# Scores of the first batch as plain float32 products, and a later place for VectorE's conversion of three weight pieces

## The chip, the core and the metric

One core of a Trainium2 chip runs the whole kernel. The metric is the device time of one execution in microseconds (us). Its engines are TensorE (PE; its weight loads are PEld), VectorE (DVE), ScalarE (ACT), GpSimd (POOL) and SyncE (SP), which here issues every DMA. Each engine takes its instructions in the order in which they stand in its own queue.

## What is computed

Three stages follow each other: attention with a decay, a gated feed-forward layer, and eight expert layers with a balanced gate.

```python
scores = scale * np.matmul(q, k.transpose(0, 1, 3, 2))      # 4 batches, 8 heads, 576 x 576, head size 64
decay  = cum[:, :, :, None] - cum[:, :, None, :]            # cum: running sum of log f
scores = np.where(causal, -1e9, scores + decay)
attn   = softmax(scores)                                    # max, exp, sum, divide
x      = np.matmul(attn, v)                                 # -> (2304, 512)
x      = (silu(x @ w_gate) * (x @ w_val)) @ w_out           # first feed-forward layer, 512 -> 1536 -> 512
out    = sum over 8 experts e of P[:, e] * (relu(x @ w1[e]) @ w2[e])
```

The change is in the scores of batch 0 and in when a part of `w_gate`, `w_val` and `w_out` is prepared.

## The kernel before

**Order.** The program writes lists of steps (`attn_unit`, `moe_unit`) and `merge` (L21) interleaves two lists by their costs. Then a scheduler puts the instructions of each engine into a fixed order. L475 merges the attention of batch 0 with the conversion of the first three weight pieces; L476 merges the attention of batch 1 with the first feed-forward layer of batch 0, which converts 15 more pieces as it needs them; the later stages follow in the same way. A unit of the feed-forward layer needs all four pairs of heads of its batch, since it sums over 512 features, 128 from each pair.

**A head of attention.** `load` (L227) fetches q and k of one head, transposed, as 64 partitions (head size) by 2 x 576 columns. It fetches them twice, into partitions 0 to 63 and 64 to 127 (L230). ScalarE rounds all of it to the reduced float32 format fp32r (L247, tile `qkh`); GpSimd then replaces the lower half of q by the rest that rounding left (L249), and writes the rest of k to `kl` (L250). So one product over 128 partitions gives (q high + q low) times k high, and a second one with `kl` adds the rest of k. `cb` holds the decay sums, repeated over 128 partitions; that of the very first head is made by TensorE and ScalarE (L238, L241), the others are fetched.

`scores` (L256) takes 128 query rows at a time (five tiles; the last in two chunks of 288 columns). For a chunk TensorE makes the product with `kh` (L268, at least 256 columns wide), adds a causal mask by a bfloat16 product with the identity (L271, on the chunk that ends at the diagonal), and makes the product with `kl` (L272). VectorE adds the decay and takes the minimum in one pass to tile `np` (L274), ScalarE takes the exponential (L278). `trans` (L301) transposes the tile by TensorE (L309), and VectorE or ScalarE copies it out (L313). `pv` multiplies it with v (L332): in batch 0 as plain float32, which shows as two matmul records for each product. `fold` (L346) divides by the sums of a pair of heads: a row goes out to DRAM and comes back repeated (L292, L297), and GpSimd multiplies (L350).

**A weight piece.** `convert` (L98) turns one of 18 pieces of 1 MB, stored as 64-bit floats, into a high and a low fp32r part. A DMA fetches it to `st` (L103; two buffers), VectorE, ScalarE and VectorE again compute on the words (L111, L113, L114, L116, L117: four VectorE steps), GpSimd adds (L122), ScalarE and GpSimd write the two parts to `w` (L124, L142), and a DMA stores them for the later batches (L126). Before the change nothing but the scheduler decides where the four VectorE steps stand among the score rows.

Of the kernel before, what the change touches and what calls it, by code (L numbers as in the profile page):

```python
# [8 lines left out]
F32 = mybir.dt.float32  # L9
F32R = mybir.dt.float32r  # L10
# [10 lines left out]
def merge(*streams, lead=1.0):  # L21

    at = [0.0] * len(streams)
    total = [(sum(c for c, _ in s) or 1.0) * (1.0 if n else lead) for n, s in enumerate(streams)]
    left = [list(s) for s in streams]
    while any(left):
        i = min((at[n] / total[n], n) for n in range(len(left)) if left[n])[1]
        cost, step = left[i].pop(0)
        at[i] += cost
        step()  # L30
# [3 lines left out]
def attention_two_ffns(ctx: ExitStack, tc: tile.TileContext, qkT, vt, f, wf, g2, w1, w2, out):  # L34
    nc = tc.nc
    B, H, D, _, S = qkT.shape
# [4 lines left out]
    P = 128  # L41
# [7 lines left out]
    def pool(name, bufs, **kw):  # L49
        return tc.tile_pool(name=name, bufs=bufs, **kw)  # L50
# [14 lines left out]
    identb = const.tile([P, P], BF16, name="identb")  # L65
# [3 lines left out]
    maskb = const.tile([P, P], BF16, name="maskb")  # L69
# [28 lines left out]
    def convert(i):  # L98
        base = bases[:, 1:2] if i % 3 == 2 else bases[:, 0:1]
        W = 2 * HP  # L100
        st = cvp.tile([P, 4 * W + 4], U16, tag="st", name="st", bufs=2)
        with tc.issue_after(last_qk[0].ins) if i < PACE else ExitStack():
            nc.sync.dma_start(out=st[:, 1:1 + 4 * W], in_=wf[i].bitcast(U16))  # L103

        def words(dt):
            return st.bitcast(dt)[:, 0:2 * W].rearrange("p (i t) -> p i t", t=2)[:, :, 1]
        mid, v = words(U32), words(F32)
        top = st[:, 4:4 + 4 * W].rearrange("p (i t) -> p i t", t=4)[:, :, 0]
        y = cvp.tile([P, W], U16, tag="y", name="y")
        g = cvp.tile([P, W], U16, tag="g", name="g")  # L110
        nc.vector.tensor_scalar(out=y, in0=top, scalar1=0x7fff, scalar2=None, op0=ALU.bitwise_and)  # L111

        nc.scalar.activation(out=g, in_=y, func=AF.Relu, scale=8.0, bias=base)  # L113
        nc.vector.scalar_tensor_tensor(  # L114
            out=g, in0=top, scalar=0x8000, in1=g, op0=ALU.bitwise_and, op1=ALU.bitwise_or)
        nc.vector.tensor_scalar(out=y, in0=g, scalar1=0xff80, scalar2=None, op0=ALU.bitwise_and)  # L116
        nc.vector.scalar_tensor_tensor(  # L117
            out=v, in0=mid, scalar=2.0**-36, in1=y.bitcast(BF16), op0=ALU.mult, op1=ALU.mult)
        t = wring.tile([P, 2, 2, HP], F32R, tag="w", name="w")
        halves = [slice(j * HP, (j + 1) * HP) for j in range(2)]  # L120
        for h in halves:
            nc.gpsimd.tensor_tensor(out=v[:, h], in0=v[:, h], in1=g[:, h].bitcast(BF16), op=ALU.add)  # L122
        for j, h in enumerate(halves):
            nc.scalar.copy(out=t[:, j, 0], in_=v[:, h])  # L124
            rest(t[:, j, 1], v[:, h], t[:, j, 0])
        nc.sync.dma_start(out=wsplit[i], in_=t.bitcast(F32))  # L126
        return t

    last_dma = [None]
    last_qk = [None]  # L130
    NPE = 1
    PACE = 2
    ONV = (2, 4)

    def fetch(i):
        t = wring.tile([P, 2, 2, HP], F32R, tag="w", name="w")
        last_dma[0] = nc.sync.dma_start(out=t.bitcast(F32), in_=wsplit[i])
        return t

    def rest(out, src, hi, eng=None):  # L140

        (eng or nc.gpsimd).tensor_tensor(out=out, in0=src, in1=hi.bitcast(F32), op=ALU.subtract)  # L142
# [14 lines left out]
    raw = at_ctx.enter_context(pool("raw", 2, side="right"))  # L157
    spl = at_ctx.enter_context(pool("spl", 2, side="right"))
# [3 lines left out]
    small = at_ctx.enter_context(pool("small", 1, side="right"))  # L162
# [40 lines left out]

    def attn_unit(b):
        first = b == 0
        pairs, heads = {}, {}

        def load_pair(hp):
            if hp == 0:
# [15 lines left out]
            pairs[hp] = vs, btp.tile([P, S], F32, tag="bt", name="bt", bufs=2)  # L225

        def load(h):  # L227
            qk = raw.tile([P, 2, S], F32, tag="qk", name="qk")
            src = qkT[b, h]
            for half in (slice(0, 64), slice(64, P)):  # L230
                last_qk[0] = nc.sync.dma_start(out=qk[half], in_=src)
            cb = raw.tile([P, S], F32, tag="cb", name="cb")
            r = b * H + h
            if r < NPE:

                for c0 in (0, HB):
                    ps = ps_t.tile([P, 512], F32, tag="t", name="ps_c")
                    nc.tensor.matmul(  # L238
                        out=ps[:, 0:HB], lhsT=ident[0:B * H, r:r + 1].to_broadcast([B * H, P]), rhs=ct[:, c0:c0 + HB],
                        start=True, stop=True)  # L240
                    nc.scalar.copy(out=cb[:, c0:c0 + HB], in_=ps[:, 0:HB])  # L241
            else:
                nc.sync.dma_start(out=cb, in_=cumd[r:r + 1, :].to_broadcast([P, S]))
            qkh = spl.tile([P, 2, S], F32R, tag="qkh", name="qkh")
            kl = spl.tile([P, S], F32R, tag="kl", name="kl")
            a, kh = qkh[:, 0], qkh[:, 1]
            nc.scalar.copy(out=qkh, in_=qk)  # L247

            rest(a[64:128], qk[64:128, 0], a[64:128])  # L249
            rest(kl, qk[:, 1], kh)  # L250
            mn = small.tile([P, 6], F32, tag="mn", name="mn", bufs=4)
            heads[h] = a, kh, kl, cb, mn, {}
            if h % 2 == 0:
                load_pair(h // 2)

        def scores(h, qi):  # L256
            a, kh, kl, cb, mn, nps = heads[h]
            sm, col = sms[h // 2 % 2], (h % 2 * 4 + qi if qi < 4 else 8 + h % 2)
            last = qi == 4
            qs, r0 = (448, 64) if last else (qi * P, 0)  # L260
            L = min((qi + 1) * P, S)
            pt = npp.tile([P, L], F32, tag=f"np{qi}", name="np")
            nps[qi] = pt
            chunks = ((0, 288, 288), (288, 288, 288)) if last else ((0, max(L, 256), L),)
            prev = 3.0e38
            for n, (c0, w, use) in enumerate(chunks):
                ps = (ps_m if first else ps_s).tile([P, 512], F32, tag="m" if first else "s", name="ps_s")
                nc.tensor.matmul(out=ps[:, 0:w], lhsT=a[:, qs:qs + P], rhs=kh[:, c0:c0 + w], start=True, stop=False)  # L268
                if c0 + use == L:
                    m0 = qs - c0  # L270
                    nc.tensor.matmul(out=ps[:, m0:m0 + P], lhsT=identb, rhs=maskb, start=False, stop=False)  # L271
                nc.tensor.matmul(out=ps[:, 0:w], lhsT=a[:, qs:qs + P], rhs=kl[:, c0:c0 + w], start=False, stop=True)  # L272
                m = mn[r0:P, qi + n:qi + n + 1]
                nc.vector.tensor_tensor_reduce(  # L274
                    out=pt[r0:P, c0:c0 + use], in0=ps[r0:P, 0:use], in1=cb[r0:P, c0:c0 + use], scale=-SCALE,
                    scalar=prev, op0=ALU.add, op1=ALU.min, accum_out=m)
                prev = m
            nc.scalar.activation(  # L278
                out=pt[r0:P, 0:L], in_=pt[r0:P, 0:L], func=AF.Exp, scale=-1.0, bias=prev,
                accum_out=sm[r0:P, col:col + 1])  # L280
# [20 lines left out]
        def trans(h, qi):  # L301
# [9 lines left out]
            if first:  # L311
                copy = nc.vector.tensor_copy if qi in ONV else nc.scalar.copy
                copy(out=pts[qi // 2 > 0][h % 2][:, 0:n, c:c + w], in_=pv)  # L313
# [40 lines left out]
        def head_a(h):  # L354
            scores(h, 0)
            scores(h, 1)
            trans(h, 0)
            trans(h, 1)
            pv(h, 0)

        def front_b(h):
            for t in (2, 3, 4):
                scores(h, t)
# [7 lines left out]
        for h in range(H):  # L371
            steps += [(c, lambda fn=fn, h=h: fn(h)) for c, fn in
                      ((0.3, load), (1.5, head_a), (2.0, front_b), (2.0, back_b))]
            if h % 2 == 1:
                steps.append((0.3, lambda hp=h // 2: fold(hp)))
# [3 lines left out]
    def group(w):  # L379
        return [w[0][:, 0], w[1][:, 0]], [w[0][:, 1], w[1][:, 1]], [w[2][:, 0], w[2][:, 1]]  # L380
# [91 lines left out]

    LA, LB, LC = 1.0, 1.2, 1.2
    w0 = []
    merge(attn_unit(0), [(1.0, lambda i=i: w0.append(convert(i))) for i in range(3)])  # L475
    merge(attn_unit(1), moe_unit(0, convert, group(w0)), lead=LA)  # L476
    merge(attn_unit(2), moe_unit(1), lead=LB)
    merge(attn_unit(3), moe_unit(2), lead=LC)
    at_ctx.close()
# [275 lines left out]
```

## Time and profile before

| | |
|---|---|
| median of 3 runs | 2271.68 us (2269.86 to 2273.07) |
| span of the profiled execution | 2267.1 us; its own time is not printed apart from the three runs, whose median lies 4.6 us over the span |
| TensorE busy | 2224.7 us, 98% of the span |
| VectorE, ScalarE, GpSimd busy | 1689.3 us (75%), 852.1 us (38%), 887.4 us (39%) |
| moved by DMA | 232.5 MB, 103 GB/s on average |

The span goes from the first to the last instruction. A busy TensorE is an average over stages: in the first stages, in which attention and conversion run, it has its gaps. A matmul's record is longer than the time after which the next one starts, because matmuls are pipelined; what a matmul costs in a stream is read from one start to the next.

### The profile page before, as it was taken

The numbers are of one execution on the slowest core, as the hardware profiler recorded it, in microseconds if no ns is written. First come the engines' busy times: TensorE is split into PE (matmuls) and PEld (weight loads), VectorE is DVE, ScalarE is ACT, GpSimd is POOL, SyncE is SP. The second block draws the span as 40 slices with busy tenths as digits, with TensorE's granted clock in tenths as the row PEclk, the third lists the DMA queues.
The fourth block names the chain that finished last, engine by engine and source line by source line (L and its number), as shares of the span: only waits on it lengthen the run. The fifth ranks groups of instructions, "written<-read, shape, count | busy, mean of one in ns | idle before, by whom it ended". The sixth has DMA issues, their size and how long they took to land.

```text
span 2267.1 us, 36323 instructions
## 1 busy us (share of the span) xinstructions
PE 2224.7 (98%) x13881; PEld 2020.8 (89%) x13881; DVE 1689.3 (75%) x3385; ACT 852.1 (38%) x1952; POOL 887.4 (39%) x684
## 2 busy tenths in 40 slices
PE   7898999999999999999999999999999999999999
PEld 5698899999999888898988989889989899898897
DVE  6778854544535799887888878877788787887876
ACT  7866754454322434332322323223232232322321
POOL 6869863342423444332323323333233232332320
PEclk9999999999999999999999999999999999999999
DMA  9766664454644232111111111161111111111101
GB/s 249 204 204 217 217 228 159 164 170 146 236 161 154 89 119 94 59 56 38 47 47 38 56 38 47 49 224 56 38 47 47 38 56 38 47 47 38 56 29 52
DMA packets 105102, 232.50 MB, mean 103 GB/s; under 512 B 10672, under 2 KB 60128, under 8 KB 92896
## 3 DMA queue, kind: packets, MB, share of 16 engines
q1 hardware_dynamic: 104928, 230.18, 31.5%
q8 instruction: 109, 1.79, 0.3%
q14 instruction: 65, 0.53, 0.1%
HBM read 193.27 MB, written 36.87 MB: 102 GB/s over the span
## 4 chain that ended last, share of the span: by engine, by line
PE 85%; DMA 6%; DVE 5%; POOL 1%; ACT 1%; issue 1%; SPq 1%; POOLq 0%; DVEq 0%; ACTq 0%
PE py L150 39%; PE pa L601 30%; PE pm L150 10%; DMA st<-wf 3%; PE ps_o L340 1%; PE ps_t L309 1%; PE ps_s L272 1%; DMA xst<-xd 1%; PE ps_s L268 1%; DMA rb<-rd 1%; DVE al L616 1%; DVE np L274 0%; DMA rd<-rt 0%; DVE y L111 0%; DMA lgd<-ls 0%
## 5 line engine op out<-in xcount | busy, mean ns | idle before, releaser
L601 PE MATMUL pa<-xf,w1h 128*128 128x288 f32 x3584 | 748.8, 295 | 0.2 <-DVE u L610 0.2
L601 PEld LDWEIGHTS pa<-xf,w1h 128*128 128x128 f32 x3584 | 597.7, 188 | 37.8 <-DVE u L610 0.7
L653 DVE SCALAR_TENSOR_TENSOR acc<-py,lg,acc 128x512 f32<-128x512 f32 x531 | 395.2, 744 | 247.5 <-PE py L150 247.3
L601 PE MATMUL pa<-xf,w1l 128*128 128x288 f32 x1792 | 527.6, 295 | 0.0
L142 POOL TENSOR_TENSOR w2l<-w,w2h 128x1024 fp32r<-128x1024 f32 x64 | 154.6, 2416 | 820.5 <-ACT w2h L577 820.5
L150 PE MATMUL py<-w2h,ah 128*128 128x512 f32 x1152 | 454.2, 394 | 3.3 <-DVE acc L646 2.8
L150 PE MATMUL py<-w2l,ah 128*128 128x512 f32 x1152 | 454.1, 394 | 0.0
L150 PE MATMUL py<-w2h,al 128*128 128x512 f32 x1152 | 453.2, 393 | 0.0
L616 DVE SCALAR_TENSOR_TENSOR al<-c,ah 128x288 fp32r<-128x288 f32 x512 | 431.5, 870 | 5.4 <-ACT ah L615 4.7
L615 ACT ACTIVATE ah<-c 128x288 fp32r<-128x288 f32 x512 | 208.0, 443 | 566.4 <-PE py L150 319.5
L601 PEld LDWEIGHTS pa<-xf,w1l 128*128 128x128 f32 x1792 | 337.0, 188 | 10.6
L150 PE MATMUL pm<-xh,w 128*128 128x288 f32 x1536 | 326.3, 298 | 3.3 <-DVE xa L431 1.6
L150 PEld LDWEIGHTS py<-w2h,al 128*128 128x128 f32 x1152 | 216.3, 188 | 50.0
L150 PEld LDWEIGHTS pm<-xh,w 128*128 128x128 f32 x1536 | 252.0, 188 | 6.2 <-DVE xa L431 2.1
L150 PEld LDWEIGHTS py<-w2h,ah 128*128 128x128 f32 x1152 | 216.3, 188 | 32.6 <-DVE acc L646 3.2
L150 PEld LDWEIGHTS py<-w2l,ah 128*128 128x128 f32 x1152 | 216.3, 188 | 26.1
L150 PE MATMUL pm<-xl,w 128*128 128x288 f32 x768 | 226.2, 295 | 0.5 <-POOL xl L142 0.5
L621 ACT COPY m<-pa 128x288 f32<-128x288 f32 x128 | 50.3, 393 | 437.0 <-PE pa L601 434.8
L142 POOL TENSOR_TENSOR w1l<-w,w1h 128x256 fp32r<-128x256 f32 x192 | 162.3, 873 | 125.1 <-ACT w1h L573 125.1
L150 PE MATMUL py<-ah,w 128*128 128x288 f32 x768 | 174.6, 299 | 4.8 <-DVE th L413 2.5
L142 POOL TENSOR_TENSOR al<-th,ah 128x288 fp32r<-128x288 f32 x96 | 83.6, 871 | 203.0 <-ACT ah L415 200.7
L142 POOL TENSOR_TENSOR w1l<-sm,w1h 128x1024 fp32r<-128x1024 f32 x64 | 153.7, 2401 | 2.5 <-ACT w1h L573 2.5
(145 smaller groups left out, 3109.4 us busy)
## 6 DMA issues: line engine op xcount, KB each, us to landing
w<-w SPq DMA_DIRECT2D x128, 512.0 KB, 3.5
w<-wsplit SPq DMA_DIRECT2D x54, 1024.0 KB, 5.5
qk<-qkT SPq DMA_DIRECT2D x64, 288.0 KB, 6.2
st<-wf SPq DMA_DIRECT2D x18, 1024.0 KB, 8.7
wsplit<-w SPq DMA_DIRECT2D x18, 1024.0 KB, 4.7
cb<-cumd SPq DMA_DIRECT2D x31, 288.0 KB, 4.0
xo<-h SPq DMA_DIRECT2D x28, 288.0 KB, 2.2
xf<-xo SPq DMA_DIRECT2D x14, 576.0 KB, 10.1
```

The lines of the kernel that those rows point to most:

```text
L142: (eng or nc.gpsimd).tensor_tensor(out=out, in0=src, in1=hi.bitcast(F32), op=ALU.subtract)
L150: nc.tensor.matmul(out=ps, lhsT=a, rhs=b, start=(i == 0), stop=(i == n - 1))
L268: nc.tensor.matmul(out=ps[:, 0:w], lhsT=a[:, qs:qs + P], rhs=kh[:, c0:c0 + w], start=True, stop=False)
L272: nc.tensor.matmul(out=ps[:, 0:w], lhsT=a[:, qs:qs + P], rhs=kl[:, c0:c0 + w], start=False, stop=True)
L309: nc.tensor.transpose(pv[:, j, :], pt[r0:P, k0:k0 + P], ident[r0:P, r0:P])
L340: nc.tensor.matmul(out=po[:, c0:w], lhsT=vs[:, j, e].rearrange("p a d -> p (a d)"), rhs=pts[rng][part][:, j, c0:w], start=(i == 0), stop=( ...
L601: nc.tensor.matmul(out=ps, lhsT=w[:, MW[m - 1], k], rhs=x[:, m - 1, hl, k], start=(n == 0), stop=(n == len(ops) - 1))
L615: nc.scalar.activation(out=ah[:, f, tk], in_=src, func=AF.Relu)
L616: nc.vector.scalar_tensor_tensor(out=al[:, f, tk], in0=src, scalar=0.0, in1=ah[:, f, tk].bitcast(F32), op0=ALU.max, op1=ALU.subtract)
L621: nc.scalar.copy(out=m1, in_=p1)
L653: nc.vector.scalar_tensor_tensor(out=a, in0=py, scalar=lg[:, t, e:e + 1], in1=a, op0=ALU.mult, op1=ALU.add)
```

## The change

Batch 0 no longer splits q and k. `load` fetches a head's q and k once, an even head into partitions 0 to 63 and the odd one into 64 to 127 of one tile, and keeps no `qkh` and no `kl`. `scores` makes one float32 product over these 64 partitions for each chunk, no wider than needed, and the mask. The other batches are as before. The four VectorE steps of the first three pieces are tied behind the last score row (`np`) that was written down before them, and empty steps move the pieces along the merged list.

```diff
+        hold = ExitStack()
+        if i < NW0:
+            hold.enter_context(tc.issue_after(last_np[0].ins))
...
             out=v, in0=mid, scalar=2.0**-36, in1=y.bitcast(BF16), op0=ALU.mult, op1=ALU.mult)
+        hold.close()
...
+    last_np = [None]
+    NW0 = 3
...
+    EXACT = 1
...
+        exact = b < EXACT
...
-            qk = raw.tile([P, 2, S], F32, tag="qk", name="qk")
+            if h % 2 == 0 or not exact:
+                qk = qks[0] = raw.tile([P, 2, S], F32, tag="qk", name="qk")
+            qk = qks[0]
             src = qkT[b, h]
-            for half in (slice(0, 64), slice(64, P)):
+            rows = slice(64 * (h % 2), 64 * (h % 2) + 64)
+            for half in (rows,) if exact else (slice(0, 64), slice(64, P)):
                 last_qk[0] = nc.sync.dma_start(out=qk[half], in_=src)
...
+            if exact:
+                heads[h] = qk[rows, 0], qk[rows, 1], None, cb, mn, {}
+            else:
+                qkh = spl.tile([P, 2, S], F32R, tag="qkh", name="qkh")
...
-                nc.tensor.matmul(out=ps[:, 0:w], lhsT=a[:, qs:qs + P], rhs=kh[:, c0:c0 + w], start=True, stop=False)
-                if c0 + use == L:
+                masked = c0 + use == L
+                if exact:
+                    w = use
+                nc.tensor.matmul(
+                    out=ps[:, 0:w], lhsT=a[:, qs:qs + P], rhs=kh[:, c0:c0 + w], start=True, stop=exact and not masked)
+                if masked:
...
-                nc.tensor.matmul(out=ps[:, 0:w], lhsT=a[:, qs:qs + P], rhs=kl[:, c0:c0 + w], start=False, stop=True)
+                if not exact:
+                    nc.tensor.matmul(
+                        out=ps[:, 0:w], lhsT=a[:, qs:qs + P], rhs=kl[:, c0:c0 + w], start=False, stop=True)
                 m = mn[r0:P, qi + n:qi + n + 1]
-                nc.vector.tensor_tensor_reduce(
+                last_np[0] = nc.vector.tensor_tensor_reduce(
...
-    merge(attn_unit(0), [(1.0, lambda i=i: w0.append(convert(i))) for i in range(3)])
+    merge(attn_unit(0), [x for i in range(NW0) for x in ((0.4, lambda: None), (1.0, lambda i=i: w0.append(convert(i))))])
```

On VectorE's queue the first head stands so before the change (`ct` is the decay sum, `y`, `g`, `st` are steps of a weight piece, `np` are score rows, each with a row that reads its minimum `mn`):

```order
L178 TENSOR_SCALAR ct<-ct 32x576
L111 TENSOR_SCALAR y<-st 128x1024
L274 ISA np,mn<-ps_s,cb 128x128
L274 ISA mn 128x1
L274 ISA np,mn<-ps_s,cb 128x256
L274 ISA mn 128x1
L274 ISA np,mn<-ps_s,cb 128x384
L274 ISA mn 128x1
L114 SCALAR_TENSOR_TENSOR g<-st,g 128x1024
```

and so with the change (its lines are 3 to 20 higher):

```order
L185 TENSOR_SCALAR ct<-ct 32x576
L294 ISA np,mn<-ps_s,cb 128x128
L294 ISA mn 128x1
L294 ISA np,mn<-ps_s,cb 128x256
L294 ISA mn 128x1
L294 ISA np,mn<-ps_s,cb 128x384
```

The first step of piece 0 moves from ahead of the first score row to behind the last one of head 0. In the same way the steps of piece 1 now stand behind head 3 and those of piece 2 behind head 6; before, they stood around head 1 and around heads 3 and 4.

On TensorE's queue the program begins so before the change (`ps_c` is the decay of the first head):

```order
L238 MATMUL ps_c<-ct,ident 128x288 x2
L268 MATMUL ps_s<-qkh 128x256
L271 LDWEIGHTS identb
L271 MATMUL ps_s<-maskb,identb 128x128
L268 MATMUL ps_s<-qkh 128x256
```

and so with the change:

```order
L285 MATMUL ps_s<-qk 128x128
L289 LDWEIGHTS identb
L289 MATMUL ps_s<-maskb,identb 128x128
L285 MATMUL ps_s<-qk 128x256
L289 LDWEIGHTS identb
L289 MATMUL ps_s<-maskb,identb 128x128
L285 MATMUL ps_s<-qk 128x384
L289 LDWEIGHTS identb
L289 MATMUL ps_s<-maskb,identb 128x128
L249 MATMUL ps_c<-ct,ident 128x288 x2
```

Three score chunks now stand ahead of `ps_c`, and each product over 64 partitions (`qk`) stands between masks, transposes or products over 128 partitions. Up to the last float32 product with v, TensorE's queue changes from 128 to 64 partitions 16 times before and 57 times with the change.

At the end of batch 0, VectorE's queue with the change has the steps of pieces 2 and 3 among the score rows of head 7 (this is a stretch of it):

```order
L333 COPY pt<-ps_t 128x5x64
L114 TENSOR_SCALAR y<-st 128x1024
L117 SCALAR_TENSOR_TENSOR g<-st,g 128x1024
L294 ISA np,mn<-ps_s,cb 128x512
L294 ISA mn 128x1
L294 ISA np,mn<-ps_s,cb 64x288
L294 ISA mn 64x1
L119 TENSOR_SCALAR y<-g 128x1024
L117 SCALAR_TENSOR_TENSOR g<-st,g 128x1024
L294 ISA np,mn<-ps_s,cb,mn 64x288
L294 ISA mn 64x1
L120 SCALAR_TENSOR_TENSOR st<-st,y 128x1024
```

Before, pieces 2 and 3 stood apart, around heads 3 and 4 and around heads 5 and 6.

## Rows read from the trace of the kernel before

**Rows 1.** The page's busy times by engine.

```profile
PE 2224.7 (98%) x13881; PEld 2020.8 (89%) x13881; DVE 1689.3 (75%) x3385; ACT 852.1 (38%) x1952; POOL 887.4 (39%) x684
```

**Rows 2.** Busy time by stretch: window length, engines with counts, PEclk, DMA share, GB/s.

```profile
14.00:79.50 65.50, 57.25 (x311) 43.95 (x312) 51.84 (x132) 55.60 (x134) 53.40 (x37) 0.92 0.90 252
68.10:71.50 3.40, 3.40 (x15) 2.62 (x13) 1.66 (x10) 2.49 (x8) 3.40 (x3) 0.50 1.03 371
79.50:113.20 33.70, 30.02 (x174) 23.30 (x172) 24.65 (x64) 25.38 (x64) 25.68 (x21) 0.95 0.64 181
150.00:330.00 180.00, 168.70 (x1203) 155.03 (x1202) 139.77 (x318) 118.15 (x276) 144.54 (x115) 0.98 0.69 227
```

**Rows 3.** What TensorE waited for from 0 to 125 us: total, times, longest.

```profile
PE ps_s L268 <- DVE mn L274: 8.6, 6, 2.8
...
PE ps_s L272 <- POOL kl L142: 1.8, 1, 1.8
```

**Rows 4.** VectorE in order of time: start, duration, instruction, idle before.

```profile
13.37 0.69 DVE L111 TENSOR_SCALAR y<-st 128x1024 uint16<-128x1024 uint16 x1 [6.71 <-DMA st<-wf]
13.98 0.28 DVE L274 CUSTOM_DVE_ANT_0 np<-ps_s,cb 128x128 f32<-128x128 f32 x1
...
74.91 1.44 DVE L111 TENSOR_SCALAR y<-st 128x1024 uint16<-128x1024 uint16 x1 [3.02 <-DMA st<-wf]
...
79.50 0.29 DVE L274 CUSTOM_DVE_ANT_0 np<-ps_s,cb 128x128 f32<-128x128 f32 x1
```

**Rows 5.** Groups by form, 0 to 93 us: busy us, mean ns, idle before.

```profile
L142 POOL TENSOR_TENSOR kl<-qk,qkh 128x576 fp32r<-128x576 f32 x10 | 18.0, 1798 | 0.8
...
L247 ACT CAST qkh<-qk 128x1152 fp32r<-128x1152 f32 x11 | 12.6, 1149 | 1.9 <-DMA qk<-qkT 1.9
```

**Rows 6.** TensorE in order of time, around 57 us.

```profile
56.17 0.39 PE L268 MATMUL ps_s<-qkh 128*128 128x512 f32 x1
...
56.76 0.29 PE L268 MATMUL ps_s<-qkh 128*128 128x288 f32 x1
56.89 0.30 PE L272 MATMUL ps_s<-kl,qkh 128*128 128x288 f32 x1
...
57.13 0.82 PE L332 MATMUL ps_o<-pt,vs 128*128 128x256 f32 x4
...
57.92 0.23 PE L271 MATMUL ps_s<-maskb,identb 128*128 128x128 bf16 x1
```

**Rows 7.** TensorE in order of time, around matmuls over 64 partitions (64*128).

```profile
31.16 0.29 PE L272 MATMUL ps_s<-kl,qkh 128*128 128x288 f32 x1
31.38 0.53 PE L309 MATMUL ps_t<-ident,np 64*128 64x64 f32 x5
31.83 0.40 PE L268 MATMUL ps_s<-qkh 128*128 128x288 f32 x1
32.07 0.23 PE L271 MATMUL ps_s<-maskb,identb 128*128 128x128 bf16 x1
...
125.96 0.27 PE L309 MATMUL ps_t<-ident,np 64*128 64x64 f32 x1
126.16 0.28 PE L288 MATMUL ps_r<-ident,rc 128*10 128x128 f32 x1
```

**Rows 8.** TensorE in order of time, at the program's start.

```profile
6.80 2.25 PE L238 MATMUL ps_c<-ct,ident 32*128 32x288 f32 x4 [6.80 <-DVE ct L178]
...
14.33 0.80 PE L268 MATMUL ps_s<-qkh 128*128 128x512 f32 x1 [2.25 <-DVE mn L274]
```

**Rows 9.** VectorE's four steps of a piece by form, 0 to 93 us.

```profile
L114 DVE SCALAR_TENSOR_TENSOR g<-st,g 128x1024 uint16<-128x1024 uint16 x6 | 10.7, 1777 | 0.4 <-ACT g L113 0.4
L117 DVE SCALAR_TENSOR_TENSOR st<-st,y 128x1024 f32<-128x1024 uint32 x5 | 9.0, 1796 | 0.2
...
L111 DVE TENSOR_SCALAR y<-st 128x1024 uint16<-128x1024 uint16 x6 | 5.9, 991 | 12.5 <-DMA st<-wf 12.5
...
L116 DVE TENSOR_SCALAR y<-g 128x1024 uint16<-128x1024 uint16 x5 | 5.0, 990 | 0.1
```

More of the change, by code (lines that the diff above doesn't have):

```diff
@@ L205, in attn_unit @@
         first = b == 0
-        pairs, heads = {}, {}
+        exact = b < EXACT
+        pairs, heads, qks = {}, {}, [None]
         def load_pair(hp):
@@ L243, in load @@
                 nc.sync.dma_start(out=cb, in_=cumd[r:r + 1, :].to_broadcast([P, S]))
[L244 to L250, printed above, removed]
-            mn = small.tile([P, 6], F32, tag="mn", name="mn", bufs=4)
-            heads[h] = a, kh, kl, cb, mn, {}
+            mn = small.tile([P, 6], F32, tag="mn", name="mn", bufs=4)
+            if exact:
+                heads[h] = qk[rows, 0], qk[rows, 1], None, cb, mn, {}
+            else:
+                qkh = spl.tile([P, 2, S], F32R, tag="qkh", name="qkh")
+                kl = spl.tile([P, S], F32R, tag="kl", name="kl")
+                a, kh = qkh[:, 0], qkh[:, 1]
+                nc.scalar.copy(out=qkh, in_=qk)
+                rest(a[64:128], qk[64:128, 0], a[64:128])
+                rest(kl, qk[:, 1], kh)
+                heads[h] = a, kh, kl, cb, mn, {}
             if h % 2 == 0:
@@ L267, in scores @@
                 ps = (ps_m if first else ps_s).tile([P, 512], F32, tag="m" if first else "s", name="ps_s")
-                nc.tensor.matmul(out=ps[:, 0:w], lhsT=a[:, qs:qs + P], rhs=kh[:, c0:c0 + w], start=True, stop=False)
-                if c0 + use == L:
+                masked = c0 + use == L
[4 more added lines that the diff above has]
+                if masked:
                     m0 = qs - c0
-                    nc.tensor.matmul(out=ps[:, m0:m0 + P], lhsT=identb, rhs=maskb, start=False, stop=False)
-                nc.tensor.matmul(out=ps[:, 0:w], lhsT=a[:, qs:qs + P], rhs=kl[:, c0:c0 + w], start=False, stop=True)
+                    nc.tensor.matmul(out=ps[:, m0:m0 + P], lhsT=identb, rhs=maskb, start=False, stop=exact)
+                if not exact:
+                    nc.tensor.matmul(
+                        out=ps[:, 0:w], lhsT=a[:, qs:qs + P], rhs=kl[:, c0:c0 + w], start=False, stop=True)
                 m = mn[r0:P, qi + n:qi + n + 1]
-                nc.vector.tensor_tensor_reduce(
+                last_np[0] = nc.vector.tensor_tensor_reduce(
                     out=pt[r0:P, c0:c0 + use], in0=ps[r0:P, 0:use], in1=cb[r0:P, c0:c0 + use], scale=-SCALE,
```

## Prediction

> **What bounds the kernel now.** I read the page's busy times first. TensorE is busy for 98% of the span [rows 1], so over the whole program the time is TensorE's work plus what it loses, and a change must be judged by both. Then I read busy time by stretch, to see where it loses anything. From 14.0 us (the first score row of batch 0 on VectorE) to 79.5 us (the first of batch 1) [rows 4], TensorE is busy 57.25 of 65.5 us at a mean granted clock of 0.92; up to 113.2 us it is busy 30.02 of 33.7 at 0.95 [rows 2]. Between 150 and 330 us, where attention of the next batch, conversion and the first feed-forward layer share the engines, it still loses 11.3 us [rows 2]. The change touches batch 0 and three weight pieces, so the first two stretches decide.
>
> Third, the waits. TensorE's largest is for VectorE's score rows, 8.6 us in six waits, and another is for the rest of k from GpSimd, 1.8 us [rows 3]. Fourth, VectorE in order of time shows where its score rows were: behind the first step of a weight piece whose data had not landed. Piece 0 held the queue for 6.71 us until 13.37, and later a piece held it for 3.02 us until 74.91 [rows 4]. After such gaps TensorE's granted clock falls: from 68.1 to 71.5 us it is 0.50, the lower of its two levels (1.2 and 2.4 GHz) [rows 2]. So in batch 0 TensorE has slack: 8.25 us without work and 8% of 65.5, or 5.2 us, lost to the clock.
>
> **The change part by part.** First, more columns. Before, a head has six chunks of 256, 256, 384, 512, 288 and 288 columns, each multiplied twice: 3968 columns. A 288-column fp32r matmul takes 0.13 us from start to start (56.76 to 56.89) [rows 6], 0.45 ns per column: 1.79 us. Now it is 128 + 256 + 384 + 512 + 576 = 1856 columns in float32. The four float32 records of 256 and 128 columns that start at 57.13, with one 288-column matmul behind them, last until 57.92; without its 0.13 that is 0.66 us for 384 columns [rows 6], 1.72 ns per column: 3.19 us. A head costs 1.40 us more, eight heads **+11.2 us**.
>
> Second, changes of partitions. The new products run over 64 partitions, among others over 128. Five transposes over 64 take from 31.38 to 31.83, 0.45 us; a single one takes 0.20 (125.96 to 126.16), so each further one costs 0.06 [rows 7]. From 31.16 to 32.07 there are two 288-column matmuls (0.26) and those five (0.31): 0.57 us of work in 0.91 [rows 7]. One visit to 64 partitions thus costs 0.34 us. The order has 41 more of them. A part was already paid: a masked 512-column chunk takes 0.59 us from 56.17 to 56.76, where two matmuls at 0.45 ns per column take 0.46 [rows 6], so some 0.13 goes to the mask and its own change of weights, which now falls together with the visit. I take 0.20 a visit, **+8.2 us**; the ends are 0 (long matmuls hide the change of weights, which no row shows) and 0.34, or 13.9. I stay nearer to the row than to 0 because every visit in the trace pays it.
>
> A rule of the Trainium skill speaks against the change here: TensorEngine Tiling (Array Packing), Key Properties, says "Mode switching requires drain". The trace agrees that a switch costs something [rows 7]; read strictly, with a drain for each of the 41, the term would be 13.9 in place of 8.2, and that is the third rival below.
>
> Third, the start. The first score row waited for piece 0 until 13.98 [rows 4]. Now it needs a score chunk and the decay of head 0. The decay's four matmuls, 2.25 us [rows 8], stand behind three chunks of 768 columns together: 1.32 us, double at the low rate of the start (512 columns last 0.80 us there against 0.39 later [rows 8, 6]), so 2.6. From 6.7 us, when q and k must have landed, with some 0.4 for masks and 0.9 until half of the decay is copied, the first row can come near 11.5: **-2.5 us**. It can't come before 9.5 (the decay right at 6.8 and its 2.25 us) nor, by this, later than before. The slow matmuls of the start now lie earlier, in time that was waited away: I take **-2.0**, between 0 and 4.
>
> Fourth, the waits in batch 0. Steps of pieces 0 to 2 now come when their data is there, and no `kl` is waited for. TensorE has more work for each head while ScalarE loses a 1.15 us rounding and GpSimd 1.80 us for the rest of k (and as much again for q's, nearly) [rows 5], so the others come early more often. Of 8.25 us without work I keep 2.5: **-5.8**, and with the gaps goes the low clock: **-5.2**. The ends are nothing recovered and all of it. These removed instructions, and half of the q and k transfers, are costed at nothing by themselves: they lie beside TensorE, and count only through these waits.
>
> Fifth, from 79.5 to 113.2 us, 3.7 us without work and 1.7 to the clock [rows 2]. Piece 2 and those after it are converted about a head later than before, so VectorE has more to do there, while GpSimd starts it without a backlog. I take **-1.5**, between +2 and -4. Later stretches have the same work in nearly the same order: 0.
>
> The sum is 11.2 + 8.2 - 2.5 - 2.0 - 5.8 - 5.2 - 1.5 = +2.4 us on the span of 2267.1. The median of the runs lies 4.6 us over that span, which I leave as it is: 2271.7 + 2.4, or **2274 us**. More work of TensorE takes the place of its waits, and little is left over either way. A measurement of this kernel can tell about 0.2%, or 4.5 us, from no change.
>
> **The rivals.** *Faster: the visits are hidden.* The price of 0.34 comes from matmuls of 64 columns, shorter than a load of weights; behind 256 and more float32 columns such a load could run unseen. Then the 8.2 us fall away: 2266 us, and with a kept wait less some 2264. For it: the new products are long. Against it: what each visit loses on the 288-column matmul before it is seen too (0.22 from 31.16 to 31.38, where 0.13 is usual [rows 7, 6]).
>
> *Slower: VectorE becomes the bound at the end of batch 0.* A piece costs VectorE 1.78 + 1.80 + 0.99 + 0.99 = 5.55 us [rows 9]. From 14 to 79.5 it is busy 51.84 us [rows 2], of which four pieces take 22.2; the rest is 3.7 us for each of eight heads. In the new order pieces 2 and 3 stand together among heads 6 and 7: 11.1 + 7.3 = 18.4 us, where TensorE needs two heads at about 8.9, or 17.8. It decides from the point where VectorE needs more than TensorE, and it does by 0.6. Then the score chunks wait for their PSUM buffers, as they did after 74.91. Two stops of some 2 us, each followed by 3.4 us at half clock (1.7 lost, as at 68.1 [rows 2]), give 7.4: 2281 us. Against it: in the rest of batch 0 VectorE has less to do than before.
>
> *Slower: every visit is paid in full*, 0.34 each: 5.7 us more, 2280 us. It holds if the mask and the float32 products don't share their changes of weights.
>
> **How the numbers follow.** The forecast, TensorE's new work and the recovered waits nearly equal, has 0.37: its own range is 2269 to 2276. The hidden visits have 0.28, since the largest uncertain term could vanish whole and nothing else adds work. VectorE as the bound has 0.22: two engines within 0.6 us of each other. Full visits have 0.13, since the row shows a price, yet a part of it was already paid. So faster 0.28, same 0.37, slower 0.35. The range goes down to 2263 (no cost of visits and no kept wait: 2274 - 8.2 - 2.5) and up to 2286 (full visits, +5.7, and half of the 11 us of waits and clock not recovered, +5.5, and a little of the fifth term).
>
> **What would show it.** Right: from the first score row of batch 0 to that of batch 1 TensorE is busy nearly throughout at clock 1.00, the six waits for `np` shrink to one or two, the first row comes near 11.5 us and batch 1 starts between 80 and 85. A float32 chunk of 512 columns takes about 0.9 us from start to start, and a mask between two chunks loses another 0.1 to 0.3. The first rival shows as masks and neighbours that lose nothing, with batch 1 before 77 us; the second as TensorE waiting for `np` near heads 6 and 7 with VectorE busy on `g` and `st`; the third as batch 1 after 86 us without waits. The prediction is wrong if batch 0 ends at the same time and the difference arises beyond 113 us, where I expect none.

## The result, and the profile after

The changed kernel takes 2284.38 us (median of 4 runs, 2282.94 to 2288.74) against 2272.38 for the kernel before on the same chip: a ratio of 1.007, with an interval of 1.0053 to 1.0087. It is **slower**: the medians lie 12.0 us apart, and the ratio on record, 1.007, stands for some 16 us. Measured again later, beside other kernels, the ratio was 1.008 (1.0065 to 1.0096). The forecast was 2274, within 0.2% of before; 2284 lies inside the range that was given, on the slower side.

The page of the changed kernel, busy times; [rows 1] answers to it:

```profile
PE 2245.0 (98%) x13881; PEld 2021.8 (89%) x13881; DVE 1682.9 (74%) x3385; ACT 847.0 (37%) x1944; POOL 861.0 (38%) x668
```

TensorE has 20.3 us more of busy time, and the share is 98% as before. The same kernel by stretch; [rows 2] answers to it:

```profile
14.00:79.50 65.50, 64.88 (x287) 37.68 (x286) 41.33 (x109) 42.37 (x107) 18.76 (x14) 1.00 0.55 165
81.50:84.90 3.40, 3.40 (x9) 2.25 (x9) 2.69 (x6) 2.14 (x8) 2.23 (x3) 0.50 0.62 156
79.50:113.20 33.70, 30.05 (x169) 22.64 (x169) 23.07 (x70) 27.17 (x68) 26.64 (x23) 0.94 0.77 232
150.00:330.00 180.00, 165.33 (x1187) 152.24 (x1186) 145.58 (x319) 120.83 (x279) 147.81 (x115) 0.98 0.66 214
```

In batch 0 TensorE now works nearly throughout. The clock of 1.00 is right only from 23.5 us on; before that its matmuls ran at half rate, which the page does not print (last section). From 79.5 to 113.2 us nothing is gained, and from 150 to 330 us it is without work for 14.7 us, where before it was 11.3. What TensorE waited for from 0 to 125 us, the four largest (total, times, longest), against [rows 3]:

```profile
PE ps_s L285 <- DMA qk<-qkT: 5.5, 1, 5.5
PE ps_t L329 <- DVE pt L333: 2.5, 1, 2.5
PE ps_s L285 <- DVE mn L294: 2.2, 2, 1.8
PE pm L157 <- ACT xh L371: 0.7, 1, 0.7
```

The six waits of 8.6 us for score rows have become two of 2.2. The first row of batch 0 and the first of batch 1 on VectorE, against [rows 4]:

```profile
11.38 0.29 DVE L294 CUSTOM_DVE_ANT_0 np<-ps_s,cb 128x128 f32<-128x128 f32 x1 [4.76 <-ACT cb L252]
...
90.27 0.29 DVE L294 CUSTOM_DVE_ANT_0 np<-ps_s,cb 128x128 f32<-128x128 f32 x1
```

The first comes at 11.38 (forecast 11.5); batch 1 begins at 90.27, before at 79.50 (forecast 80 to 85).

**Where the time went.** To set work against loss I took, for each kind of matmul and of its follower, the usual time from start to start at full clock in these traces, and summed it along TensorE's records: that is the work. The start time less the work done by then is the loss: waits and low clock together. Each row is one execution. The work, and with it the loss up to 90 us, is good to some 4 us, since it depends on which value is called usual; the loss behind 90 us, where all kernels have the same shapes, to some 2. The ratio is that of the kernel's runs to those of before on its chip. (The kernels e1 to e14 are the experiments.)

```
kernel               ratio    work    loss to 90 us   loss from there to the end
before               1        2178.5       33.4            51.1
the change           1.007    2200.5       18.1            59.9
the change again     1.008    2200.5       23.8            59.1
e1 hold only         0.9975   2179.9       27.3            47.5
e2 float32 only      1.002    2203.1       19.7            45.4
e3 128 partitions    0.9995   2184.6       21.2            53.8
e4 one fp32r product 1.0011   2186.2       32.7            50.9
e5 four ties         1.0016   2200.7       14.5            51.7
e6 one tie           0.9997   2201.6       19.2            42.8
e7 128, no tie       0.9963   2183.9       24.3            50.4
e8 128, one tie      0.9993   2184.1       20.9            56.3
e10 space 0.6        1.0038   2200.4       17.5            53.7
e11 128, four ties   0.9987   2184.7       22.0            54.2
e12 as before, 1 tie 1.0011   2178.8       34.9            49.1
e13 space 0.3        1.0046   2201.3       21.0            54.5
e14 space 0.2        1.0049   2200.7       19.3            57.0
```

The change adds some 22 us of work. It takes 15.3 us of loss out of the first 90 us (9.6 in the other execution) and puts 8 to 9 us in behind them, where the forecast had a gain of 1.5 and then nothing.

### The profile page after: what moved, and what is told of

It reads as the page before. It is cut to its first block, busy times and chain, and to the rows that moved or that the text cites. A ratio compares the mean times of both kernels' runs of the same rounds, so it can differ in the third digit from the quotient of the medians.

```text
span 2282.6 us, 36254 instructions
## 1 busy us (share of the span) xinstructions
PE 2245.0 (98%) x13881; PEld 2021.8 (89%) x13881; DVE 1682.9 (74%) x3385; ACT 847.0 (37%) x1944; POOL 861.0 (38%) x668
## 4 chain that ended last, share of the span: by engine, by line
PE 87%; DVE 4%; DMA 4%; POOL 2%; issue 2%; ACT 1%; SPq 0%; POOLq 0%; DVEq 0%; ACTq 0%
PE py L157 39%; PE pa L621 30%; PE pm L157 11%; PE ps_s L285 2%; PE ps_t L329 2%; PE ps_o L360 1%; PE ps_o L352 1%; DMA st<-wf 1%; PE ps_s L291 1%; DMA rb<-rd 1%; DMA qk<-qkT 1%; POOL w L149 1%; PE ps_s L289 0%; DMA lgd<-ls 0%; DVE np L294 0%
```

## The experiments

### Each half alone, and the scores without their two costs

*e1 hold only*: `EXACT = 0`. *e2 float32 only*:

```diff
-        if i < NW0:
+        if i < 0:
...
-    merge(attn_unit(0), [x for i in range(NW0) for x in ((0.4, lambda: None), (1.0, lambda i=i: w0.append(convert(i))))])
+    merge(attn_unit(0), [(1.0, lambda i=i: w0.append(convert(i))) for i in range(3)])
```

*e3 128 partitions* (each head has a tile of its own):

```diff
-            rows = slice(64 * (h % 2), 64 * (h % 2) + 64)
+            rows = slice(0, 64)
+            if exact:
+                nc.gpsimd.memset(qk[64:128], 0.0)
...
-                heads[h] = qk[rows, 0], qk[rows, 1], None, cb, mn, {}
+                heads[h] = qk[:, 0], qk[:, 1], None, cb, mn, {}
```

*e4 one fp32r product*:

```diff
-                heads[h] = qk[rows, 0], qk[rows, 1], None, cb, mn, {}
+                qkh = spl.tile([P, 2, S], F32R, tag="qkh", name="qkh")
+                nc.scalar.copy(out=qkh[rows], in_=qk[rows])
+                heads[h] = qkh[rows, 0], qkh[rows, 1], None, cb, mn, {}
...
-                if exact:
-                    w = use
```

> Scores of batch 0 as before the change (two fp32r products over 128 partitions), and only VectorE's later place for pieces 0 to 2. Theory A (TensorE's added work costs some 15 to 20 us in batch 0 and the later place of the pieces gives a part of it back): the place alone gains. The first score row comes near 12.0 us instead of 13.98, the waits for score rows fall from 8.6 us to under 3, batch 1's first score row comes at 70 to 75 us instead of 79.5, and the time is 2262 to 2268 us. Rival B (the place itself costs, since two pieces then meet at the end of batch 0 and the stretch behind it has a later start of the conversion): 2272 us or more, with batch 1's first score row not before 78.

> Float32 scores over 64 partitions, with the pieces where they stood before the change (VectorE's steps are not tied to score rows). Theory A: the added work of TensorE is there and VectorE's early stop for piece 0 stays (first score row not before 13.4 us), so batch 1's first score row comes at 91 to 95 us (90.27 with the whole change, 79.50 before) and the time is 2286 to 2292 us. Rival B (the new place of the pieces makes the loss): faster than the whole change, 2276 us or less.

> As the whole change, but every head has its own tile of q and k in partitions 0 to 63, GpSimd writes zeros to partitions 64 to 127, and the score products run over all 128 partitions: the same columns in float32, no change of partitions. Theory A1 (41 visits to 64 partitions cost 0.25 to 0.34 us each): batch 1's first score row comes 8 to 13 us earlier than the 90.27 of the whole change, and the time is 2271 to 2276 us. Rival A2 (the float32 columns and the low clock make the loss, visits are hidden behind long products): no more than 3 us earlier, 2281 to 2285 us; a 512-column chunk with its mask still takes 1.06 us from start to start and the masks still 0.16 us.

> As the whole change, but q and k are rounded to fp32r by ScalarE (over 64 partitions) and multiplied once; the low parts of q and k are left out, so the scores are coarser. The visits to 64 partitions stay, and 1856 float32 columns a head (1.67 ns each, 3.1 us) become 1984 fp32r columns (0.45 ns each, 0.9 us). Theory A1 (columns and visits both count in full): 2.2 us less a head, batch 1's first score row at 71 to 75 us and the time 2265 to 2270 us. Rival A2 (visits hide only behind the long float32 products and come out when these are short): 1.2 us less a head or under, batch 1's first score row at 79 us or later, 2273 us or more.

**e1**: 2263.35 us, 0.9975 (0.9965 to 0.9985), faster than before by some 6 us, as theory A had it. The first score row came at 12.06 and the waits for rows fell to 0.7 us. But batch 1 began at 81.5, not at 70 to 75: when batch 1 begins does not tell the time. The scheduler moves other work past that point: by then TensorE had done 18 products of the feed-forward layer, before the change 7.

**e2**: 1.002 (1.0012 to 1.0029), 2273.38 us. Batch 1 begins at 94.6, as theory A said, and yet the kernel is not at 2286 or above: it lost 45.4 us behind 90 us, where the change lost 59.9. The time is rival B's (2276 us or less), the late start of batch 1 is theory A's, and neither holds as a whole: the place that B blames gains in e1. One half gains 6 us, the other costs 4.5, together they cost 16: **the halves don't add up**, and what does not is, by the table, loss and not work.

**e3**: 0.9995 (0.9985 to 1.0006), 2268.37 us: theory A1, and a little below its numbers. Batch 1 begins at 79.35. By the table 15.9 of the 22.0 us of added work are gone with the change of partitions, and the float32 columns leave 6.1; the rows make it less. A chunk of 512 columns, its mask and what follows, in the change and then in e3 (TensorE in order of time):

```profile
52.06 1.12 PE L285 MATMUL ps_s<-qk 64*128 64x512 f32 x2
53.12 0.23 PE L289 MATMUL ps_s<-maskb,identb 128*128 128x128 bf16 x1
53.28 0.75 PE L285 MATMUL ps_s<-qk 64*128 64x288 f32 x2
```

```profile
51.15 1.08 PE L287 MATMUL ps_s<-qk 128*128 128x512 f32 x2
52.07 0.22 PE L291 MATMUL ps_s<-maskb,identb 128*128 128x128 bf16 x1
52.12 0.70 PE L287 MATMUL ps_s<-qk 128*128 128x288 f32 x2
```

From the start of the chunk to the mask 1.06 against 0.92 us, from the mask to the next chunk 0.16 against 0.05: 0.25 us for the same columns. Over 48 chunks that is 12 us, or 0.29 for each of the 41 visits of the prediction; the table's 15.9 would be 0.33 and 0.39. Either is nearer to the 0.34 of [rows 7] than to the 0.20 taken, beside long float32 products too; the first rival, that these hide it, is out. The Trainium skill (TensorEngine Tiling (Array Packing), Key Properties) says that a change of tiling mode drains TensorE; the trace agrees that a chunk among such changes costs more, by these 0.25 us. They fall on both records of the chunk (0.53 and 0.52 us from start to start, in e3 0.49 and 0.43) and on the way from the mask to the next chunk.

**e4**: 1.0011 (0.9994 to 1.0027), 2271.26 us, and batch 1 at 90.0: the start of batch 1 is rival A2's, the time lies between the two. The work says theory A1: 14.3 us less than the change by the table, 1.8 a head, near its 2.2. A 512-column chunk in e4 (TensorE in order of time):

```profile
70.83 0.50 PE L285 MATMUL ps_s<-qkh 64*128 64x512 f32 x1
71.26 0.23 PE L289 MATMUL ps_s<-maskb,identb 128*128 128x128 bf16 x1
71.42 0.40 PE L285 MATMUL ps_s<-qkh 64*128 64x288 f32 x1
```

To the mask it takes 0.43 us, in the change 1.06, and from the mask to the next chunk 0.16 as there. What was saved went to the clock, for 27 us in a row (window length, busy times, granted clock, DMA share, GB/s):

```profile
36.00:64.00 28.00, 26.78 (x81) 15.98 (x80) 13.80 (x41) 20.14 (x49) 7.29 (x6) 0.52 0.58 170
```

So the columns count on TensorE, the visits are paid beside short products as beside long ones, and in this execution the work that was saved came back as low clock. It took 2275.74 us, among eleven from 2260.18 to 2279.38.

### The place of the pieces

> The whole change, with piece 3 tied as well, behind the last score row of batch 0, so that pieces 2 and 3 no longer stand together on VectorE among heads 6 and 7. Theory C (that meeting costs about 4 us, a stop of 2.5 us and a slow clock behind it, and nothing else hangs on it): the stop near 80 us is gone, batch 1's first score row comes at 85 to 87 us instead of 90.27, and the time is 4 us under the whole change, about 2280 us (ratio to before 1.005). Theory D (what is lost behind batch 0, 8 us more than before, comes from weight pieces that are converted too late): piece 3 is later still, so the gain at 90 us is given back by 350 us and the time is 2284 us or more (ratio 1.007 or more).

> The whole change, but only piece 0 is tied to a score row; pieces 1 and 2 stand where the scheduler puts them, and no empty steps lie between the pieces. Theory D (pieces too late cost behind batch 0): six pieces are done when batch 1 starts, as with float32 scores alone, so the loss behind 90 us falls back by 8 us or more and the time is 2268 to 2274 us. Rival (the loss behind batch 0 is not set by where the first pieces stand): 2280 us or more.

> Float32 scores over 128 partitions (zeros below), and no piece tied (as before the change). The partitions' price, 15 us of TensorE's work, and the place of the pieces, 11 us between the whole change and float32 scores alone, are apart if they add up: 2273 - 15 = 2258 us. Theory D (place matters by itself): 2255 to 2262. Rival (the place cost only because the batch was long and full; with a shorter one TensorE waits for VectorE again): 2266 us or more, as before the change.

> Float32 scores over 128 partitions (zeros below), with piece 0 alone tied behind the score rows of head 0 and the others free. Theory D: neither VectorE's early stop nor the late pieces: 2252 to 2260 us, under both kernels and under the later place alone (2263). Rival (no gain over all three tied): 2266 us or more.

Their edits: *e5* `if i < NW0 + 1:`, *e6* `if i < 1:` with the three pieces behind a single empty step of 0.3; *e7* is e3 with e2's edit, *e8* e3 with e6's.

The second rival named the place: in the change VectorE's steps for pieces 2 and 3 stand among each other at heads 6 and 7. The changed kernel there, VectorE and then TensorE:

```profile
70.62 2.43 DVE L117 SCALAR_TENSOR_TENSOR g<-st,g 128x1024 uint16<-128x1024 uint16 x1
...
74.80 1.21 DVE L117 SCALAR_TENSOR_TENSOR g<-st,g 128x1024 uint16<-128x1024 uint16 x1
...
76.61 2.17 DVE L120 SCALAR_TENSOR_TENSOR st<-st,y 128x1024 f32<-128x1024 uint32 x1
78.68 1.62 DVE L119 TENSOR_SCALAR y<-g 128x1024 uint16<-128x1024 uint16 x1
80.33 0.96 DVE L333 COPY pt<-ps_t 128x384 f32<-128x384 f32 x2
```

```profile
78.61 0.27 PE L308 MATMUL ps_r<-ident,rc 128*10 128x128 f32 x1
81.34 0.35 PE L329 MATMUL ps_t<-ident,np 128*128 128x128 f32 x1 [2.46 <-DVE pt L333]
```

Two steps in a row, 3.7 us, stand in front of a copy for which TensorE waits 2.46 us; then its clock is at 0.50 for 3.4 us (81.5 to 84.9, shown above), 1.7 lost: about 4 us, one stop where the rival had priced two. The second execution has the same stop, and behind it 14 us at half clock (TensorE, then window length, busy times, granted clock, DMA share, GB/s):

```profile
87.26 0.47 PE L329 MATMUL ps_t<-ident,np 128*128 128x128 f32 x1 [2.46 <-DVE pt L333]
```

```profile
87.00:101.00 14.00, 13.74 (x36) 7.99 (x37) 5.92 (x19) 9.15 (x21) 11.88 (x12) 0.51 0.31 83
```

And it goes on. Both pieces reach GpSimd together with the remainders for batch 1: it works from 76.27 us on with one break of 1.17, ends piece 2 at 90.41 and piece 3 at 97.31. On SP's queue the store of piece 2 (`wsplit`) stands behind loads of batch 1, and behind it the fetch of piece 4. GpSimd, SP and VectorE of the change:

```profile
89.09 1.32 POOL L149 TENSOR_TENSOR w<-st,w 128x512 fp32r<-128x512 f32 x1
...
96.02 1.29 POOL L149 TENSOR_TENSOR w<-st,w 128x512 fp32r<-128x512 f32 x1
100.48 1.41 POOL L149 TENSOR_TENSOR qkh<-qk,qkh 64x576 fp32r<-64x576 f32 x1 [3.17 <-ACT qkh L262]
```

```profile
93.30 0.53 SPq L130 DMA_DIRECT2D wsplit<-w  x1
93.88 0.43 SPq L103 DMA_DIRECT2D st<-wf  x1
```

```profile
81.76 1.76 DVE L120 SCALAR_TENSOR_TENSOR st<-st,y 128x1024 f32<-128x1024 uint32 x1
...
103.28 0.69 DVE L114 TENSOR_SCALAR y<-st 128x1024 uint16<-128x1024 uint16 x1
```

For 20 us, from 83.5 to 103.28, VectorE converts nothing; before the change piece 4 began at 74.91 [rows 4]. VectorE's very last conversion step, in the change and before:

```profile
300.06 1.78 DVE L120 SCALAR_TENSOR_TENSOR st<-st,y 128x1024 f32<-128x1024 uint32 x1
```

```profile
286.95 1.74 DVE L117 SCALAR_TENSOR_TENSOR st<-st,y 128x1024 f32<-128x1024 uint32 x1
```

**e5** takes the two apart. Its fetch and first step of piece 4, and its first two stretches:

```profile
86.48 2.00 SPq L103 DMA_DIRECT2D st<-wf  x1
```

```profile
94.99 1.60 DVE L114 TENSOR_SCALAR y<-st 128x1024 uint16<-128x1024 uint16 x1
```

```profile
14.00:79.50 65.50, 65.50 (x288) 38.03 (x288) 38.90 (x114) 43.07 (x114) 19.95 (x15) 1.00 0.55 168
79.50:113.20 33.70, 32.00 (x190) 24.03 (x188) 27.61 (x72) 28.24 (x68) 31.25 (x25) 1.00 0.89 251
```

There is no stop, and no low clock but that of the start (until 24.2 us), the work is the same (2200.7), and the time is 2272.85 us, 1.0016 (1.0006 to 1.0027): 12 us of the change's 16 are gone by one more tie. Theory C had expected 4 us, theory D none. The stop was as C had it, 3.6 us of loss up to 90 us; but two thirds of the gain lie behind 90 us (59.9 to 51.7 of loss), and there C had expected nothing. Batch 1 begins at 88.9, only 1.4 us earlier.

**e6**: 0.9997 (0.9986 to 1.0007), 2269.44 us, with the whole work of the float32 scores: theory D's number. VectorE begins the last step of the sixth piece at 97 us, when batch 1 has begun (93.8), and the loss behind 90 us is 42.8. **e7**: 0.9963 (0.995 to 0.9976), 2261.88 us, within theory D's range, and faster than both kernels. **e8**: 0.9993 (0.9983 to 1.0003), 2267.91 us, a miss for theory D and as its rival had it: with six pieces done early it lost 56.3 us behind 90 us. How early the pieces are done does not settle that loss.

### Is it the pair, the gap behind it, or the order?

> The whole change once more, unaltered, beside the three below on one chip, as their common measure. Expected: ratio to before 1.005 to 1.009, as measured first; were it under 1.003, the 12 us between it and the version with piece 3 tied would not be an effect of the edit but of the day.

> The whole change with wider spaces between the pieces (0.6 for 0.4): pieces 2 and 3 stand step by step beside each other on VectorE, from head 6 on (both first steps behind its last score row), and the next piece comes not before head 2 of batch 1. Theory P (two pieces together stop VectorE's score rows, then fill GpSimd, and the fetch of the next piece comes late, which costs some 4 us in batch 0 and 7 behind it): at least as slow as the whole change, ratio 1.006 to 1.011. Rival (the gain from tying piece 3 came from elsewhere in the new order): 1.003 or less.

> Float32 scores over 128 partitions (zeros below), with pieces 0 to 2 tied as in the change and piece 3 tied behind the last score row of batch 0. There too pieces 2 and 3 stood among each other at heads 6 and 7. Theory P: less loss by 90 us and behind it, 4 to 12 us under the version without the fourth tie (ratio 0.9995): 0.994 to 0.998. Rival (with TensorE's shorter work the pair costs nothing, or the tie comes too late): 0.999 or more.

> Scores as before the change (fp32r, 128 partitions), with piece 0 alone tied behind the score rows of head 0; the other pieces where the scheduler puts them. If the gain of the later place without float32 scores (ratio 0.9975) comes from piece 0 alone, which held the first score row back: 0.996 to 0.9985, first score row near 12 us. Rival (the ties of pieces 1 and 2 made it): 0.9995 or more.

> The whole change with the spaces at 0.3 for 0.4: VectorE's order is that of the change up to head 5; pieces 2 and 3 still stand among each other, about a third of a head earlier (first steps in front of head 6 and in it), and the next piece (4) comes in head 0 of batch 1 instead of its second head. Theory P1 (two pieces among each other cost, wherever the next one stands): ratio 1.005 to 1.010, as the change. Theory P2 (the gap behind the pair costs, 20 us in which VectorE converts nothing and the fetch of piece 4 comes late): 1.000 to 1.004. Theory S (the scheduler's order of all later work moves with any edit, and the time scatters with it): anywhere between, and the next kernel elsewhere.

> The whole change with the spaces at 0.2: piece 1 half a head earlier, pieces 2 and 3 among each other from the end of head 5 on, piece 4 at the first score row of batch 1. Theory P1: 1.005 to 1.010. Theory P2: 1.000 to 1.003, no more than the kernel with 0.3. Theory S: anywhere between, without the order that P1 or P2 gives.

Their edits: *e9* none; *e10*, *e13* and *e14* the empty steps at 0.6, 0.3 and 0.2 for 0.4; *e11* is e3 with e5's edit, *e12* e1 with e6's.

**e9** repeated the change: 1.008 (1.0065 to 1.0096), so its distance to e5 is the edit's. **e10**: 1.0038 (1.0027 to 1.0049), a miss for theory P, and at the edge of its rival: the pair stands closer, the next piece begins still later, at 111.3, and no stop came near 80 us. **e13** and **e14**: 1.0046 (1.0032 to 1.0059) and 1.0049 (1.0037 to 1.0061): the pair is kept, piece 4 begins at 106.8 and 99.0, and both are alike, below the change. In e13 VectorE still converts nothing for 19 us, so it hardly tests the gap, and its interval reaches into both theories' ranges. In e14 the gap is down to 13 us:

```profile
84.36 1.85 DVE L120 SCALAR_TENSOR_TENSOR st<-st,y 128x1024 f32<-128x1024 uint32 x1
...
98.99 0.69 DVE L114 TENSOR_SCALAR y<-st 128x1024 uint16<-128x1024 uint16 x1 [1.98 <-DMA st<-wf]
```

Theory P2 had 1.003 at most there and is out as the whole cause; theory P1 holds within the interval, at its lower end. The stop of 2.46 us (at 81 and at 87 us) stands in both executions of the change and near that place in none of e10, e13 and e14, whose ratios are 0.002 to 0.004 lower: that is 4 to 9 us, as much as the stop and the half clock behind it took in the two executions. Taken together, the five profiles of four kernels with float32 over 64 partitions and pieces 2 and 3 among each other lost 53.7 to 59.9 us behind 90 us, the three without that pair (e2, e5, e6) 42.8 to 51.7; their ratios are 1.0038 to 1.008 against 0.9997 to 1.002, and VectorE's last conversion step starts at 299.7 to 308.5 us against 291.4 to 293.9. (In e6 pieces 0 and 1 stand together, but at head 1, far from their first use.) **e11**: 0.9987 (0.9976 to 0.9998), between theory P and its rival, 0.0008 under e3 with overlapping intervals: over 128 partitions, with 12 to 16 us less work, taking the pair apart gives nothing that can be told. **e12**: 1.0011 (1.0 to 1.0021): the first tie alone does not make e1's gain; the later ones, or the spaces between the pieces, are needed for it.

**What stays open.** Shown is that the place of the pieces makes the loss behind 90 us: with the same float32 products e2, e5 and e6 lost 45.4, 51.7 and 42.8 us there, the change 59.9 and 59.1. That it is the pair, is the reading that fits best and is not shown by itself: the two groups lie only 2.0 us apart (e10 and e5), with intervals that meet (e10 and e2). Theory S is not excluded: each edit lets the scheduler order the later program anew, and e13 and the change, with pieces 0 to 3 at nearly the same heads, differ by some 5 us. Which of the later waits carries how much of the 8 to 17 us, is open too. A third buffer for `st`, which would free the fetch alone, was not run.

## Why the prediction was wrong

- **More columns (+11.2) and visits (+8.2).** Together 19.4, measured some 22: right in size as a sum. In its parts the visits were too cheap, 12 us by the rows of the chunks (15.9 by the table), and the columns a little too dear, with the 10 (or 6.1) that are left. The columns were priced against 0.45 ns a column before; but an fp32r chunk also lost time at its mask and its changes of weights, as the 0.59 us for 512 columns in [rows 6] said, and I gave that back only at the visits. The visit's upper end of 13.9 was nearer than the 8.2 that I chose; the third rival's price was about right, and its 2280 left out what followed behind 90 us. One reading on the way to 0.34 does not carry what it was used for: a 288-column product lasted 0.22 us in front of a change of weights where the partitions stay, too (57.70 to the mask at 57.92 [rows 6], before the change), so the 0.22 ahead of the transposes need not come from their partitions.

```profile
57.70 0.38 PE L268 MATMUL ps_s<-qkh 128*128 128x288 f32 x1
```

- **The start (-2.5 and -2.0).** The first row came when forecast. The rest didn't: TensorE's matmuls ran at half rate until 23.5 us in the one execution and 36.1 in the other, where before they did until 20.3. At 30 us the loss is 12.8 and 15.9 against 15.6: a gain of 2.8, or none, for the 4.5 forecast.
- **Waits (-5.8) and low clock (-5.2) of batch 0.** Right: 64.88 of 65.5 us busy, at clock 1.00 from 23.5 us on. The reason given for the low clock fits only in part: at 68.1 the clock fell before VectorE's gap that ended at 74.91, behind a wait of TensorE for a score row (1.37 us, until 67.44). With the start, 15.5 us were forecast up to batch 1, and 15.3 and 9.6 measured up to 90 us.
- **The step that failed**: "Fifth, from 79.5 to 113.2 us ... I take **-1.5**" and "Later stretches have the same work in nearly the same order: 0". In its place stand +8 to +9 us behind 90 us, besides the stop of about 4 us before. The same work was there, but not in the same order, and the order had been put at nothing: pieces 2 and 3 landed together, and the conversion ran 13 us late until 300 us. That the place of the pieces makes it, is shown; which wait carries it, stays open. With the two pieces apart (e5) the change costs 1.0016, or 3.6 us, beside a forecast of +2.4.
- **The rivals.** The second, slower by VectorE at the end of batch 0, happened at the heads it named, with one stop in place of two, and TensorE waited there for a copy of transposed rows, not for a score row; its 2281 left out what followed behind 113 us. It deserved more than 0.22: VectorE's rows and the new order gave 18.4 us of its work against 17.8 of TensorE's in those heads, and the sum of the forecast left no room for it. That 2284 lies inside the range is luck: the upper end stood for full visits and for half of batch 0's waits and clock not recovered, and those were recovered.

## What to carry to other kernels

When an edit moves work of a helper engine, follow two such pieces of work to where they land beside each other: here two pieces that had each hidden well stopped TensorE where they met, and the next fetch started late. Price a new shape against what the old one took from start to start, with its masks and weight changes, not against its columns. Products over half of the partitions may be cheaper with zeros in the other half: here 0.25 us for each chunk. Float32 scores over 128 partitions with the pieces left alone (e7, 0.9963) and the later place alone (e1, 0.9975) both beat both kernels.

## What the runs showed of the hardware

The page prints clock 1.00 for the first slices, but TensorE's matmuls ran at half rate there, and for how long differs between executions of one kernel. The change in its second execution, and in its first (TensorE):

```profile
23.00 1.65 PE L285 MATMUL ps_s<-qk 64*128 64x384 f32 x2
24.58 0.29 PE L289 MATMUL ps_s<-maskb,identb 128*128 128x128 bf16 x1
```

```profile
24.43 1.07 PE L285 MATMUL ps_s<-qk 64*128 64x512 f32 x2
25.44 0.23 PE L289 MATMUL ps_s<-maskb,identb 128*128 128x128 bf16 x1
```

384 columns take 1.58 us in the one at a time when 512 take 1.01 in the other; the records of the granted clock begin at 36.1 and at 23.5 us. The two differ by 5 to 6 us of loss by 90 us, and are a reason not to build on a single profile.

The kernels differ in it too. In the eight executions with float32 products over 64 partitions the records begin between 22.8 and 40.0 us, in the four over 128 partitions (e3, e7, e8, e11) between 13.9 and 18.1, and the matmuls change their rate there: e3 takes 1.06 us for 288 columns at 13.33 and 0.49 at 14.51, e2 still 1.26 at 32.79, where 64 partitions take 0.68 at full clock (86.91 to 87.59 in the change). TensorE in order of time, e3 and then e2:

```profile
13.33 1.24 PE L287 MATMUL ps_s<-qk 128*128 128x288 f32 x2
14.39 0.28 PE L331 MATMUL ps_t<-ident,np 128*128 128x128 f32 x1
14.51 0.65 PE L287 MATMUL ps_s<-qk 128*128 128x288 f32 x2
15.00 0.22 PE L291 MATMUL ps_s<-maskb,identb 128*128 128x128 bf16 x1
```

```profile
32.79 1.33 PE L285 MATMUL ps_s<-qk 64*128 64x288 f32 x2
34.05 0.29 PE L289 MATMUL ps_s<-maskb,identb 128*128 128x128 bf16 x1
```

So the gain of the 128-partition kernels holds an earlier full clock besides the chunks' 0.25 us. No run separates the partitions from the rest as the reason.
